# The first batch of a sliding-window attention + MLP kernel: one block of v loaded through ScalarE's queue, and two pairs' transposes moved ahead of two bias tables

## The chip, the cores and the metric

The kernel runs on one core of one Trainium2 chip. The metric is the device time of one execution in microseconds (us). A time is the median of several executions; next to it stands one execution that the hardware profiler recorded, from which all durations of single instructions come.

## What is computed

Eight batches of eight heads, 576 positions, head size 64. Each position attends to itself and the 127 positions before it, with a bias that falls linearly with distance (ALiBi). The result, 4608 tokens by 512, goes through a two-layer network with a hard-swish between.

```python
scores = scale * np.matmul(q, k.transpose(0, 1, 3, 2))
rel = pos[:, None] - pos[None, :]
bias = slopes[:, None, None] * (-np.abs(rel))[None, :, :]
mask = (rel >= 0) & (rel < 128)
scores = np.where(mask, scores + bias[None], -1e9)
attn = softmax(scores)                 # over the last axis
x = np.matmul(attn, v).transpose(0, 2, 1, 3).reshape(4608, 512)
h = x @ w_in                           # 512 x 2048
g = h * np.clip(h + 3.0, 0.0, 6.0) / 6.0
out = g @ w_out                        # 2048 x 512
```

## The kernel before

The work goes batch by batch; within a batch two heads make a pair, so a batch has four pairs, numbered g = 0 to 3 for batch 0 and g = 4 to 7 for batch 1. The order of the instructions on each engine is the order in which the program writes them out; nothing is reordered. The attention of a batch is woven into the network's matmuls of earlier tokens; batch 0 has no earlier tokens, so at the start the engines have only the attention of batch 0 to do. This start is `first_batch`.

For each pair of batch 0 the steps are these.

- `load_run` (L92) loads q or k of the pair, 288 KB each, as one row of 2304 bytes for each partition. The k runs are issued by ScalarE, the q runs by SyncE (SP): pair 0 first, then 1, 2, 3.
- `prepare(g, ...)` (L208) casts both to bf16 tiles `pr`.
- `transposes(g, ...)` (L219) turns them on TensorE with 18 small matmuls for q and 18 for k, into the PSUM tiles `tp`, and two copies (L220) bring q and k into `qTb` and `kTb`.
- `tables_diag` (L271) and `tables_off` (L307, L310) put the bias tables of the pair into PSUM by matmuls with the identity; `scores_diag` (L296) and `scores_off` (L322, L328) add the scores of the diagonal and the off-diagonal blocks on top. The two PSUM buffers of the pool `ps_sc` are taken in turn by the diagonal tile `scd`, the off-diagonal tile `sco` and later by `attend`.
- `exp_full` (L348, L335) is one exponential of 128x1024 on ScalarE for each of the two tiles.

All of v of batch 0 goes to `ldbuf` by `load_tokens(0, "v")` (L112): five blocks of tokens, four with 128 rows (256 KB each) and a last one with 64 rows (128 KB), cut into pieces of 256 bytes. All five are issued by SP, in order, right behind its four q runs. `cast_v` (L181) casts each block into `vbuf`. The first load of the network's weights, `load_w_in(0)` (L166, issued by GpSimd), stands behind `cast_v(0, 1, P)` on GpSimd's queue. P, V and A name the engine of a copy: GpSimd, VectorE, ScalarE.

Behind that stand the loads of batch 1's q and k, `load_double(1, dp, ...)` (L98): for dp = 0 and 1 two DMAs of k and two of q on SP's queue, then batch 1's v. Then come `attend(0)` to `attend(3)` (L383, L391; reciprocal and product L412, L413) with `back` (L432, L438), which transposes a pair's result into `xT`. `up_begin(0, 0, 3)` (L451) starts the network's first matmuls with three of the four pairs; it needs `w_in` of `load_w_in(0)` and the `xT` of pairs 0 to 2. `back(3)` and `wide_double(1, 0, "q", V)` (L254), the transposes of batch 1's first q, come next; the latter needs `prepare_double(1, 0, (P, P))` (L227), four casts on GpSimd, one for each of the four DMAs of dp = 0.

A DMA that SP or ScalarE issues takes the next of eight completion semaphores and waits until that semaphore's earlier DMA has landed. So the first v block waits for pair 0's k run, the second for pair 0's q run, the third for pair 1's k run, the fourth for pair 1's q run and the fifth for pair 2's k run. The wait and the issue occupy the issuing engine's queue: nothing behind them on that engine starts before.

Of the kernel before, what the change touches and what calls it, by code (L numbers as in the profile page):

```python
# [18 lines left out]
def kernel(  # L19
# [9 lines left out]
    nc = tc.nc  # L29
    B, H, S, D = q.shape  # L30
# [54 lines left out]
    src_of = {"q": q, "k": k, "v": v}  # L85
# [16 lines left out]
    def tokens(b, nm):  # L102
        if (b, nm) not in ld:
            i = 2 + b % 2 if b < 3 else (3, 1, 0, 2)[(3 * (b - 3) + "qkv".index(nm)) % 4]
            ld[b, nm] = ldbuf[i][:, 0:NQ * H * D].rearrange("p (j h d) -> p j h d", j=NQ, h=H)
        return ld[b, nm]

    def load_tokens(b, nm):
        t = tokens(b, nm)
        for j in range(NQ):  # L110
            n = min(128, S - j * 128)
            nc.sync.dma_start(out=t[:n, j, :, :],  # L112
                              in_=src_of[nm][b, :, ds(j * 128, n), :].rearrange("h p d -> p h d"))

    def constants():
        make_identity(nc, ident)
# [33 lines left out]
    def warm_up(n):  # L150
        w = ps_av.tile([128, 128], FP32, tag="av", name="w")
        for _ in range(n):
            nc.tensor.matmul(w, lhsT=ident, rhs=ident, start=True, stop=True)
# [11 lines left out]
    def load_w_in(g):  # L165
        nc.gpsimd.dma_start(  # L166
            out=w_in_sb[:, :, ts(g, 512)],
            in_=moe_w_in[:, ts(g, 512)].rearrange("(k p) f -> p k f", p=128))
# [6 lines left out]
    def second_w_in():  # L175
        nc.gpsimd.memset(w_out_sb[:, 4, 0:1], 0.0)
        load_w_in(1)

    def cast_v(b, j, copy):
        n = min(128, S - j * 128)  # L180
        copy(out=vbuf[b % 2][:n, j, :, 0:D], in_=ld[b, "v"][:n, j, :, :])  # L181
# [22 lines left out]
    def prepare(g, copies):  # L204
        for nm, copy in zip("qk", copies):
            pr = prs.tile([128, RT * D], BF16, tag=f"pr{nm}", name="pr",
                          padded_shape=[128, 2 * RT * D])
            copy(out=pr, in_=runs[nm][:, g % NP, :])  # L208
            st[g, nm] = pr

    def transposes(g, copies):
        b, hp = divmod(g, NP)
        for nm, dst, copy in (("q", qTb[b % 2], copies[0]), ("k", kTb[b % 2], copies[1])):
            src = st.pop((g, nm))
            tp = ps_h.tile([128, RT, RP], BF16, tag="h", name="tp", padded_shape=[128, 16, 64])
            for t in range(RT):
                for e in range(2):
                    r = slice(e * D, (e + 1) * D)
                    nc.tensor.transpose(tp[r, t, :], src[r, ts(t, D)], ident[r, r])  # L219
            copy(out=dst[:, hp, :, :].rearrange("p j c -> p (j c)")[:, 0:S].rearrange(  # L220
                "p (a t) -> p a t", t=RT), in_=tp.rearrange("p t a -> p a t"))
# [38 lines left out]
    def full(g):  # L260
        return g < NB_FULL * NP
# [4 lines left out]
    def tables_diag(g):  # L266
        scd = ps_sc.tile([128, 2, 512], FP32, tag="sc", name="scd")
        st[g, "scd"] = scd
        for e in range(2 if diag_tabled(g) else 0):
            t = tab[:, 2 * (g % NP) + e, 1:2, :]  # L270
            nc.tensor.matmul(scd[:, e, :].rearrange("p (j c) -> p j c", j=4), lhsT=ident,  # L271
                             rhs=t.to_broadcast([128, 4, 128]), start=True, stop=False)
# [12 lines left out]
    def scores_diag(g):  # L285
        rooms(g)
        b, hp = divmod(g, NP)
        qT, kT = qTb[b % 2][:, hp, :, :], kTb[b % 2][:, hp, :, :]
        first = not diag_tabled(g)
        if (g, "scd") not in st:  # L290
            tables_diag(g)
        scd = st[g, "scd"]
        for j in range(4):
            for e in range(2):
                r = slice(e * D, (e + 1) * D)
                nc.tensor.matmul(scd[:, e, ts(j, 128)], lhsT=kT[r, j, :],  # L296
                                 rhs=qT[r, j, :], start=first, stop=first or j == 3)

    def tables_off(g):
        hp = g % NP  # L300
        sco = ps_sc.tile([128, 2, 512], FP32, tag="sc", name="sco")
        st[g, "sco"] = sco
        if full(g):
            for e in range(2):
                h = 2 * hp + e
                t = tab[:, h, 0:1, :]
                nc.tensor.matmul(sco[:, e, 128:512].rearrange("p (j c) -> p j c", j=3),  # L307
                                 lhsT=ident, rhs=t.to_broadcast([128, 3, 128]),
                                 start=True, stop=False)
                nc.tensor.matmul(sco[:, e, 0:128].rearrange("p (s c) -> p s c", s=2),  # L310
                                 lhsT=ident, rhs=tab[:, h, :, 0:64], start=False, stop=False)
# [22 lines left out]
    def exp_off_full(g):  # L334
        nc.scalar.activation(out=st[g, "po"].rearrange("p e j c -> p e (j c)"),  # L335
                             in_=st[g, "sco"], func=ACT.Exp, scale=scale)

    def exp_full(g):
        for e in range(2):
            exp_diag(g, e)  # L340
        exp_off_full(g)

    def exp_diag(g, e):
        h = 2 * (g % NP) + e
        pd, sc = st[g, "pd"], st[g, "scd"]
        if diag_tabled(g):
            if e == 0:
                nc.scalar.activation(out=pd.rearrange("p e j c -> p e (j c)"), in_=sc,  # L348
                                     func=ACT.Exp, scale=scale)
            return  # L350
        nc.scalar.activation(out=pd[:, e, :, :].rearrange("p j c -> p (j c)"),  # L351
                             in_=sc[:, e, :], func=ACT.Exp,
                             bias=bias_d[:, h:h + 1], scale=scale)
        nc.gpsimd.affine_select(out=pd[:, e, :, :], in_=pd[:, e, :, :],  # L354
                                pattern=[[0, 4], [1, 128]], channel_multiplier=-1, base=0,
                                compare_op=ALU.is_ge, fill=0.0)
# [176 lines left out]
    V, P, A = nc.vector.tensor_copy, nc.gpsimd.tensor_copy, nc.scalar.copy  # L533
# [23 lines left out]

    def first_batch():
        prepare(0, (V, A))
        warm_up(20)  # L560
        tables_diag(0)
        tables_off(0)
        warm_up(10)
        transposes(0, (V, A))
        scores_diag(0)
        prepare(1, (P, V))
        transposes(1, (V, V))
        scores_off(0)
        exp_full(0)
        scores_diag(1)  # L570
        prepare(2, (P, P))
        tables_off(1)
        transposes(2, (V, V))
        scores_off(1)
        exp_full(1)
        scores_diag(2)
        prepare(3, (P, V))
        tables_off(2)
        transposes(3, (V, V))
        scores_off(2)  # L580
        exp_full(2)
        scores_diag(3)
        scores_off(3)
        exp_full(3)
        cast_v(0, 0, V)
        cast_v(0, 1, P)
        load_w_in(0)
        cast_v(0, 2, V)
        cast_v(0, 3, V)
        cast_v(0, 4, P)  # L590
        for dp in range(2):
            for nm in "kq":
                load_double(1, dp, nm, nc.sync)
        load_tokens(1, "v")
        attend(0)
        attend(1)
        back(0)
        attend(2)
        back(1)
        second_w_in()  # L600
        prepare_double(1, 0, (P, P))
        attend(3)
        back(2)
        up_begin(0, 0, 3)
        back(3)
        wide_double(1, 0, "q", V)
        prepare_double(1, 1, (P,), "k")
        load_w_in(2)
        prepare_double(1, 1, (P,), "q")
        load_w_in(3)  # L610
        for dp in range(2):
            for nm in "kq":
                load_double(2, dp, nm, nc.sync)
        up_begin(0, 1, 3)
        done[0] = NP
        fill(1)
        wide_double(1, 0, "k", A)
        fill(2)
# [99 lines left out]
    with tc.manual_schedule(engines=every):  # L718
        load_run(0, "k", nc.scalar)
        load_run(0, "q", nc.sync)  # L720
        load_run(1, "k", nc.scalar)
        load_run(1, "q", nc.sync)
        for g in (2, 3):
            load_run(g, "k", nc.scalar)
            load_run(g, "q", nc.sync)
        load_tokens(0, "v")
        constants()
        memsets()
        memsets_later()
        first_batch()  # L730
        second_batch()
        fill(2)
        segment(2 * NP, G, lambda g: FILLS.get(g, (1, 1, 1, 2, 0, 1, 2)))
        done[0] = G
        fill(len(units))
# [30 lines left out]
```

## Time and profile before

| | us |
|---|---|
| median of 3 executions (323.81 to 324.2) | 324.15 |
| the profiled execution, whole time | 323.38 |
| its span, first to last instruction | 321.7 |
| TensorE (PE) busy | 308.1 (96%) |
| ScalarE (ACT) busy | 195.1 (61%) |
| VectorE (DVE) busy | 172.7 (54%) |
| GpSimd (POOL) busy | 140.7 (44%) |
| granted TensorE clock | 1.000 |

The span is counted from the first instruction; 323.38 - 321.7 = 1.68 us of the profiled execution lie outside it. A busy PE is not a PE at its peak, since matmuls overlap. Where the text names a time without more, it is the time from the span's start. In the timeline a row is: start, duration, engine, line, operation, what it writes and reads, count, and in brackets how long the engine had been idle and what ended that. SPq, ACTq and POOLq are the engines' DMA-issuing instructions. In the table by stretches, "DMA share" is the mean busy share of the 16 DMA engines; packets of several queues overlap in it, so it can exceed 1.

### The profile page before, as it was taken

Reading aid. Unit: us, or ns where it says so; the run is one execution under the profiler, and the core shown is the slowest. Engines: PE = TensorE matmul, PEld = TensorE weight load, DVE = VectorE, ACT = ScalarE, POOL = GpSimd, SP = SyncE. Lnnn points to the kernel's source line nnn. Section 1 sums busy time; section 2 is a strip of 40 time slices with the busy share of each in tenths; the row PEclk is TensorE's granted clock in tenths of the full one; section 3 lists DMA queues with packets and bytes.
Section 4 is the critical chain, followed back from the end, with each engine's and each line's share of the span. In section 5 each row is a group of like instructions: output and inputs, shape, how many; then the busy total and the mean of one; then the engine's idle time right before and its main releaser. Section 6 shows DMA issues by size and latency. Waiting matters only on the chain.

```text
span 321.7 us, 7010 instructions
## 1 busy us (share of the span) xinstructions
PE 308.1 (96%) x2699; PEld 166.7 (52%) x2738; DVE 172.7 (54%) x338; ACT 195.1 (61%) x334; POOL 140.7 (44%) x249
## 2 busy tenths in 40 slices
PE   6879999999999999999999999999999999999996
PEld 5465465555555455455677644554554444444443
DVE  6657675554356555555555556555655455455510
ACT  4748976877777766666676657666764344244401
POOL 8456592683494767356745664563331000000000
PEclk9999999999999999999999999999999999999999
DMA  7999999899999999999999999932112200000112
GB/s 277 202 319 225 272 255 208 223 235 204 220 223 184 220 198 201 200 223 205 186 191 191 229 176 201 211 108 86 23 53 64 76 34 35 33 33 33 67 52 79
DMA packets 131425, 51.90 MB, mean 161 GB/s; under 512 B 118976, under 2 KB 123328, under 8 KB 131392
## 3 DMA queue, kind: packets, MB, share of 16 engines
q1 hardware_dynamic: 126160, 45.36, 67.0%
q0 software_dynamic: 4224, 4.19, 8.3%
q10 hardware_dynamic: 1008, 1.90, 1.6%
q8 instruction: 21, 0.34, 0.5%
q14 instruction: 12, 0.10, 0.1%
HBM read 36.70 MB, written 9.44 MB: 143 GB/s over the span
## 4 chain that ended last, share of the span: by engine, by line
PE 82%; DMA 5%; ACT 4%; POOL 4%; issue 2%; DVE 2%; SPq 1%; POOLq 0%
PE ops L501 35%; PE hps L451 35%; DMA ldbuf<-in_q_dram 3%; PE scd L296 2%; DMA qTb<-tbuf 2%; PE av L391 2%; PE av L383 2%; ACT r L470 2%; PE sco L328 1%; PE ops L482 1%; ACT kTb L244 1%; PE tp L254 1%; POOL tbuf L194 1%; ACT gbuf L351 1%; SPq L98 1%
## 5 line engine op out<-in xcount | busy, mean ns | idle before, releaser
L471 DVE SCALAR_TENSOR_TENSOR gbuf<-r,hps 128x512 bf16<-128x512 f32 x144 | 98.7, 687 | 102.5 <-ACT r L470 100.2
L470 ACT ACTIVATE r<-hps,bias 128x512 f32<-128x512 f32 x144 | 98.9, 689 | 89.5 <-PE hps L451 88.2
L451 PE MATMUL hps<-xT,w_in_sb 128*128 128x512 bf16 (+1 forms) x621 | 142.7, 358 | 2.3 <-DMA w_in_sb<-in_moe_w_in_dram 0.9
L501 PE MATMUL ops<-w_out_sb,gbuf 128*128 128x512 bf16 x540 | 134.2, 380 | 2.3 <-issue 1.7
L451 PEld LDWEIGHTS <-w_in_sb 128*128 128x128 bf16 x640 | 58.8, 98 | 54.8 <-DMA w_in_sb<-in_moe_w_in_dram 1.3
L501 PEld LDWEIGHTS <-gbuf 128*128 128x128 bf16 x560 | 52.2, 98 | 57.2
L354 POOL TENSOR_SCALAR_AFFINE_SELECT pd<-pd 128x512 bf16<-128x512 bf16 x48 | 29.6, 631 | 34.5 <-ACT pd L351 34.4
L364 POOL TENSOR_SCALAR_AFFINE_SELECT po<-po 128x512 bf16<-128x512 bf16 x48 | 30.1, 633 | 32.7 <-ACT po L361 32.6
L351 ACT ACTIVATE pd<-scd,bias_d 128x512 bf16<-128x512 f32 x48 | 31.6, 685 | 5.0 <-PE scd L296 3.6
L194 POOL CAST tbuf<-ldbuf 128x512 bf16<-128x512 f32 (+1 forms) x45 | 25.5, 611 | 18.7 <-DMA qTb<-tbuf 9.8
L510 DVE COPY osb<-ops 128x512 f32<-128x512 f32 x33 | 22.7, 687 | 20.3 <-PE ops L501 20.3
L361 ACT ACTIVATE po<-sco,bias_o 128x512 bf16<-128x512 f32 x48 | 33.1, 689 | 0.0
L402 DVE TENSOR_TENSOR avs<-av,rc 128x384 bf16<-128x384 f32 (+1 forms) x48 | 23.6, 491 | 1.6
L391 PEld LDWEIGHTS <-pd 128*128 128x128 bf16 x192 | 14.4, 97 | 8.3 <-issue 0.5
L383 PE MATMUL av<-vbuf,po 128*128 128x65 bf16 x192 | 18.1, 193 | 0.1
L391 PE MATMUL av<-vbuf,pd 128*128 128x65 bf16 x192 | 17.5, 194 | 0.3 <-ACT kTb L244 0.3
L383 PEld LDWEIGHTS <-po 128*128 128x128 bf16 x192 | 14.4, 98 | 3.1 <-DVE avs L402 0.5
L187 POOL CAST vbuf<-ldbuf 128x1024 bf16<-128x1024 f32 x14 | 14.3, 1040 | 3.2 <-DMA ldbuf<-in_v_dram 3.2
L367 ACT ACTIVATE p4buf<-sco,bias_d 128x64 bf16<-128x64 f32 x48 | 15.5, 324 | 0.0
L227 POOL CAST pr<-ldbuf 128x576 bf16<-128x576 f32 x20 | 12.8, 669 | 4.4 <-DMA ldbuf<-in_k_dram 3.4
L296 PE MATMUL scd<-qTb,kTb 64*128 64x128 bf16 x256 | 12.7, 219 | 1.8 <-DVE kTb L220 1.1
L296 PEld LDWEIGHTS <-kTb 64*128 64x128 bf16 x256 | 7.2, 94 | 13.5 <-issue 9.7
(96 smaller groups left out, 215.0 us busy)
## 6 DMA issues: line engine op xcount, KB each, us to landing
out_dram<-osb SPq DMA_DIRECT2D x33, 256.0 KB, 2.4
ldbuf<-in_v_dram SPq DMA_DIRECT2D x32, 256.0 KB, 5.3
ldbuf<-in_q_dram SPq DMA_DIRECT2D x20, 256.0 KB, 5.1
ldbuf<-in_k_dram SPq DMA_DIRECT2D x16, 256.0 KB, 4.6
ldbuf<-in_q_dram SPq DMA_DIRECT2D x12, 288.0 KB, 6.4
ldbuf<-in_k_dram SPq DMA_DIRECT2D x12, 288.0 KB, 6.4
w_in_sb<-in_moe_w_in_dram POOLq DMA_DIRECT2D x4, 512.0 KB, 9.2
w_out_sb<-in_moe_w_out_dram POOLq DMA_DIRECT2D x4, 512.0 KB, 11.1
```

The lines of the kernel that those rows point to most:

```text
L194: nc.gpsimd.tensor_copy(out=tbuf[:m, :, j, :], in_=s[:m, j, :, :].rearrange("p (i e) d -> p i (e d)", e=2))
L296: nc.tensor.matmul(scd[:, e, ts(j, 128)], lhsT=kT[r, j, :], rhs=qT[r, j, :], start=first, stop=first or j == 3)
L351: nc.scalar.activation(out=pd[:, e, :, :].rearrange("p j c -> p (j c)"), in_=sc[:, e, :], func=ACT.Exp, bias=bias_d[:, h:h + 1], scale=scale)
L354: nc.gpsimd.affine_select(out=pd[:, e, :, :], in_=pd[:, e, :, :], pattern=[[0, 4], [1, 128]], channel_multiplier=-1, base=0, compare_op=AL ...
L361: nc.scalar.activation(out=po[:, e, :, :].rearrange("p j c -> p (j c)"), in_=sc[:, e, :], func=ACT.Exp, bias=bias_o[:, h:h + 1], scale=scale)
L364: nc.gpsimd.affine_select(out=po[:, e, :, :], in_=po[:, e, :, :], pattern=[[0, 4], [-1, 128]], channel_multiplier=1, base=-1, compare_op=A ...
L383: nc.tensor.matmul(out_av, lhsT=po[:, e, qt % 4, :], rhs=vb[:, qt - 1, h, :], start=True, stop=False)
L391: nc.tensor.matmul(out_av, lhsT=d, rhs=vb[:, qt, h, :], start=(qt == 0), stop=True)
L451: nc.tensor.matmul(hps[:, lo:hi], lhsT=w_in_sb[:, ks, ts(ms, 128)], rhs=xT[:, ks, ds(src, hi - lo)], start=(ks == 0), stop=(ks == n_ks - 1))
L470: nc.scalar.activation(out=r6, in_=hps, func=ACT.Relu, bias=bias3[:, 0:1], scale=1.0 / 6.0)
L471: nc.vector.scalar_tensor_tensor(out=gts[nt][:, ms, :], in0=r6, scalar=1.0, in1=hps, op0=ALU.min, op1=ALU.mult)
L501: nc.tensor.matmul(ops[nt, sub], lhsT=gts[nt][:, ms, ts(sub, 128)], rhs=w_out_sb[:, ms, :], start=(ms == 0), stop=(ms == n_ms - 1))
```

## The change

Block 1 of batch 0's v is issued by ScalarE, behind its cast of pair 0's k in `prepare(0, (V, A))`; SP issues the other four, the 64-row block first. GpSimd casts the 64-row block ahead of block 1 instead of last. On TensorE `transposes(2)` is written ahead of `tables_off(1)` and `transposes(3)` ahead of `tables_off(2)`. Counts of instructions and bytes stay as they were.

In the generated program the eight semaphores fall so that ScalarE's new DMA waits until pair 1's k run has landed, and SP's four wait for pair 0's k run (64-row block), pair 0's q run (block 0), pair 1's q run (block 2) and pair 2's k run (block 3).

```diff
+    def load_block(b, nm, j, eng):
+        n = min(128, S - j * 128)
+        eng.dma_start(out=tokens(b, nm)[:n, j, :, :],
+                      in_=src_of[nm][b, :, ds(j * 128, n), :].rearrange("h p d -> p h d"))
+
     def load_tokens(b, nm):
-        t = tokens(b, nm)
         for j in range(NQ):
-            n = min(128, S - j * 128)
-            nc.sync.dma_start(out=t[:n, j, :, :],
-                              in_=src_of[nm][b, :, ds(j * 128, n), :].rearrange("h p d -> p h d"))
+            load_block(b, nm, j, nc.sync)
...
     def first_batch():
         prepare(0, (V, A))
+        load_block(0, "v", 1, nc.scalar)
+        for j in (4, 0, 2, 3):
+            load_block(0, "v", j, nc.sync)
         warm_up(20)
...
         prepare(2, (P, P))
+        transposes(2, (V, V))
         tables_off(1)
-        transposes(2, (V, V))
         scores_off(1)
         exp_full(1)
         scores_diag(2)
         prepare(3, (P, V))
+        transposes(3, (V, V))
         tables_off(2)
-        transposes(3, (V, V))
         scores_off(2)
...
         exp_full(3)
+        cast_v(0, 4, P)
         cast_v(0, 0, V)
         cast_v(0, 1, P)
         load_w_in(0)
         cast_v(0, 2, V)
         cast_v(0, 3, V)
-        cast_v(0, 4, P)
...
         for g in (2, 3):
             load_run(g, "k", nc.scalar)
             load_run(g, "q", nc.sync)
-        load_tokens(0, "v")
         constants()
```

## The prediction

> **What bounds the kernel now.** I read the page first, then the chain of waits over the first 60 us, the table by stretches of 1 us, the timeline of 4 to 24 us and SP's issues one by one. PE is busy 96% of the span, and from 24 us on nearly without a gap; the two thinnest slices on the page are the first (6) and the third (7, about 16 to 24 us). The change touches only what comes before 24 us, so the question is when that gap in slice three ends. The chain of waits there:
>
> ```profile
> 14.50 8.26 DMA ldbuf<-in_q_dram
> 22.76 0.05 issue
> 22.81 0.68 POOL pr L227
> 23.49 0.05 issue
> 23.54 0.68 PE tp L254 x9
> ```
>
> The last DMA of batch 1's first q is issued at 14.50 and lands at 22.76; GpSimd casts it (0.68), and PE's transposes start at 23.54. PE had waited once more, just before:
>
> ```profile
> 21.47 0.64 ACT L438 COPY xT<-tb 128x576 bf16<-128x576 bf16 x1 [0.53 <-PE tb L432]
> 22.37 0.60 PE L451 MATMUL hps<-xT,w_in_sb 128*128 128x512 bf16 x2 [0.94 <-DMA w_in_sb<-in_moe_w_in_dram]
> ```
>
> So three things end within 0.7 us: the xT of pair 2 (21.47 + 0.64 = 22.11), w_in (issued at 12.38, median 9.7 to landing, so 22.1), and q (22.76). PE's idle time there is 0.94 + 0.29 = 1.23 us: about what a change of the start can win, and only if all three come earlier.
>
> Why do the loads land so late? By stretches (PE, PEld, DVE, ACT, POOL busy, then clock, DMA share, GB/s):
>
> ```profile
> 11.00:12.00 1.00, 1.00 (x22) 0.41 (x16) 1.00 (x2) 0.47 (x1) 0.18 (x1) 1.00 1.29 220
> 13.00:14.00 1.00, 1.00 (x44) 0.75 (x43) 0.23 (x1) 0.85 (x1) 0.26 (x1) 1.00 0.70 144
> 14.00:15.00 1.00, 0.88 (x14) 0.31 (x12) 1.00 (x2) 0.61 (x1) 0.00 (x0) 1.00 0.84 65
> 21.00:22.00 1.00, 0.43 (x5) 0.26 (x4) 0.96 (x2) 0.53 (x1) 0.79 (x2) 1.00 1.05 400
> ```
>
> The v pieces of 256 bytes run at 220 GB/s with the engines full, the rows of 2304 bytes at 400. Between them is a hole, 144 and 65 GB/s. SP's issues tell why:
>
> ```profile
> 6.36 2.78 SPq L112 DMA_DIRECT2D ldbuf<-in_v_dram  x1
> 9.19 1.02 SPq L112 DMA_DIRECT2D ldbuf<-in_v_dram  x1
> 10.26 1.94 SPq L112 DMA_DIRECT2D ldbuf<-in_v_dram  x1
> 12.31 1.45 SPq L98 DMA_DIRECT2D ldbuf<-in_k_dram  x2
> ```
>
> The first two v blocks are issued in 0.39 and 0.65 us; the third holds SP for 2.78 (until 9.14, about when the last q run lands at 9.3), the fifth for 1.94. I read this as a full queue holding its issuer. The next loads are therefore issued only at 12.31, too late to follow v without a gap.
>
> **The change, part by part.** No instruction is added or removed.
>
> *ScalarE's new DMA.* It waits for pair 1's k run; SP's third v block had the same wait and started at 6.36. ACT is free from 4.62 + 0.67 = 5.29, and what is queued behind is pair 0's k copy:
>
> ```profile
> 6.12 0.64 ACT L220 COPY kTb<-tp 128x576 bf16<-128x576 bf16 x1 [0.82 <-PE tp L219]
> ```
>
> How long such an issue holds ACT no row shows. Low end 0.39 (first v block on SP), high end 2.78 (third). ACT's queue then holds two k runs only; SP's held three q runs at its first v block, so I take 0.39. ACT is free at 6.75, the copy starts at 6.78 (+0.66), scores_diag(0) at 7.47 instead of 6.81. Pair 1's transposes waited for a GpSimd cast until 7.48 anyway (they ran at 7.53) and now start at 7.80: +0.27.
>
> *Transposes ahead of tables.* The path from pair to pair runs through PE and DVE: scores_diag, tables_off, transposes, q copy and k copy (0.76 each), scores_diag; 9.53, 12.39, 15.25, so 2.86 us a pair. Tables_off stands between scores_diag and transposes from 9.85 to 10.39, 0.54 us. Out of the way, each of the two pairs comes 0.54 earlier. The casts they need are there: pair 2's end at 9.14, pair 3's k on DVE directly behind pair 2's k copy. What is late next is scores_off, which shifts by as much as it gains, and ACT: an exponential takes 1.02, back to back 0.92 apart (15.69 to 16.61). Following the eight through: 7.90, 8.94, 10.22, 11.80, 12.72, 14.12, 15.04, 16.18, where they were 7.25, 8.66, 9.96, 11.53, 12.83, 14.39, 15.69, 16.61. The last is 0.43 earlier: +0.27 from ACT's wait, up to -1.08 from the two moves, and ACT nearly full from 11.8 on takes back the rest. The xT of pair 2 would come at 21.68.
>
> *SP's queue.* It has 3.5 v blocks. Three blocks in all were issued by 9.14 and four by 10.21, so 3.5 by about 10, 2 us ahead of 12.20. The doubles follow: their four waits (q run 2, k run 3, q run 3, the 64-row block) are over by about 10.5, so the last q goes out near 12.5 instead of 14.50. Then the hole closes: of 13 to 15, (220 - 144) + (220 - 65) = 231 KB are regained, 1.05 us at 220 GB/s. Low end: nothing, if the slowest of the 16 DMA engines had no hole (the landing waits for all sixteen); high end 2.0, the issue's whole lead. I take 0.9: q lands at 21.9, its cast ends at 22.6.
>
> *Block 1 and GpSimd.* The cast of the 64-row block (0.87) moves from 15.80, where nothing waited behind it but the next w_in, to about 10.2, where GpSimd idles 1.69 us. Block 1 landed near 11.77 as second in SP's queue; as second in ACT's, behind the k runs (last landing about 9.6) and sharing with SP's, I expect 11.5 to 13, so w_in is issued between 12.1 and 13.6 (now 12.38). The doubles now run beside it from the start. I take 21.7 for its landing, between 21.3 (0.9 earlier, as q) and 22.6.
>
> [...]
>
> *Sum.* With xT at 21.68 and w_in at 21.7, up_begin runs at 21.8 instead of 22.37; from its start to the transposes PE needs 0.87 (22.37 to 22.80, and 0.44 for back(3)), so 22.7, q's cast 22.6 permitting, against 23.54: 0.8 us. From there PE and ACT are nearly full (PE 1.00 in each stretch of 24 to 27, ACT 7.87 of 8 in 32 to 40), so the shift stays; one DMA on the later chain (qTb from 95.37) is issued by work that shifts too. I take off 0.1 for a longer ACT issue: 0.7 us. Profiled execution 323.38 - 0.7 = 322.7, span 321.0. The median of the runs is 0.77 above the profiled one: 324.15 - 0.7 = 323.45. 0.2% of it is 0.65 us, about what a measurement of this kernel can tell from no change.
>
> **The rivals.** *Hidden (24%).* The slowest DMA engine had no hole, so q and w_in land within 0.3 of 22.76 and 22.1, and PE waits for them whatever the front does. For it: the engines are full at 9 to 12, and bytes are the same. Against: 65 GB/s at 14 to 15. Time about 324.0.
>
> *ACT is held (18%), slower.* The new issue blocks as SP's third did, because SP's own queue is full or because both share what writes descriptors. At 2.78 ACT is free at 9.14, scores_diag(0) runs at 9.86, pair 1's transposes at 10.2 (+2.66); less 1.08, the front ends about 1.6 late, xT of pair 2 at 23.7, up_begin's third matmul behind it, transposes at about 24.6: 1.1 later, 325.25. It decides from where the front is 0.7 late (w_in and q cover less than that), an issue of about 1.5 us. Against: both engines issued runs side by side from 0.81 on, 0.39 to 0.48 each.
>
> *w_in is late (12%), slower.* Block 1 shares its engines, lands at 13 or after, w_in goes out 1.2 late and shares with the doubles from its first packet; landing 23.0, PE's start 0.7 late, 324.9.
>
> **How the numbers follow.** Forecast 46%, own range 322.9 to 323.8. Most of its weight, 42 points, is beyond 0.65 us; the other 4 and the hidden case make 28% within 0.2%; the two others 30% slower. The range goes from 322.6, where the idle 1.23 us is won and w_in's next wait (0.39 at 28.39) with it, to 325.4, just beyond the held ACT.
>
> **What would show it.** ACTq's v issue at 6.3 to 6.4 with about 0.4 us, kTb's first copy near 6.8; scores_diag(2) at about 12.1 and (3) at 14.4; the last exponential of batch 0 near 16.2; SP's first double near 10.3; no stretch of 1 us under 150 GB/s between 12 and 16; up_begin near 21.8. A v issue on ACT above 1.5 us, or the first cast of q (L227) still ending after 23.4, makes the forecast wrong.

## The result, and the profile after

| | before | changed |
|---|---|---|
| median, same chip (10 runs each) | 323.69 us (322.8 to 324.29) | 325.14 us (324.08 to 325.93) |
| ratio to before | 1 | 1.0052, 95% interval 1.0038 to 1.0066 |
| the profiled execution, whole time | 323.38 | 324.08 |
| its span | 321.7 | 322.3 |
| last exponential of batch 0 starts | 16.61 | 18.56 |
| first transposes of batch 1's q start | 23.54 | 24.39 |

The change makes the kernel slower by 0.5%; the forecast was 0.7 us faster. The ratios, here and below, are worked out from all runs and are not quotients of the medians; one execution of e2 and one of e4, over 1.5% longer than the fastest of its kernel, are left out of them. The profiled execution of the changed kernel is the fastest of its ten; why the others are longer comes with experiment e4.

Read the DMA side first. The timeline of the changed kernel's issues and GpSimd's casts (start, duration, engine, line, operation, tiles, count):

```profile
6.29 0.46 ACTq L110 DMA_DIRECT2D ldbuf<-in_v_dram  x1
9.87 3.00 SPq L98 DMA_DIRECT2D ldbuf<-in_k_dram  x2
13.55 0.88 POOL L168 DMA_DIRECT2D w_in_sb<-in_moe_w_in_dram  x1
20.67 3.71 POOL L229 CAST pr<-ldbuf 128x576 bf16<-128x576 f32 x6
```

ScalarE's new issue takes 0.46 us, SP reaches the first double at 9.87 instead of 12.31, and GpSimd does six of the eight casts of batch 1's q and k in one piece from 20.67, with no wait for a load between them. The same in stretches of 1 us (behind the length of the stretch PE, PEld, DVE, ACT, POOL busy, then clock, DMA share, GB/s):

```profile
13.00:14.00 1.00, 0.88 (x35) 0.67 (x36) 0.36 (x2) 1.00 (x2) 1.00 (x2) 1.00 1.31 235
14.00:15.00 1.00, 0.00 (x0) 0.00 (x0) 0.53 (x1) 0.44 (x1) 0.43 (x1) 1.00 1.06 326
15.00:16.00 1.00, 0.72 (x13) 0.47 (x12) 0.36 (x1) 0.00 (x0) 0.00 (x0) 1.00 1.06 365
```

The hole of 144 and 65 GB/s is closed (235 and 326). But look at PE in the row of 14 to 15: 0.00, TensorE does nothing at all. The chain of waits names it:

```profile
12.99 0.33 PE scd L298 x8
13.32 0.56 PE tp L221 x27
13.88 1.40 issue
15.28 0.32 PE tp L221 x9
...
23.21 0.65 ACT xT L440
23.86 0.04 issue
23.90 0.38 PE hps L453
24.28 0.28 PE tb L434 x5
24.56 0.50 PE tp L256 x9
```

In the middle of `transposes(3)`, after 27 of 36, TensorE stops for 1.40 us. "issue" means that it waited for nothing that the profile shows: no semaphore, no tile. All 36 transposes belong to one pair, and their source casts were over. From there the whole front is late: the third matmul of `up_begin` now starts at 23.90 behind the xT of pair 2 (23.21 + 0.65), where in the kernel before it was ready at 22.11, and the chain no longer holds a load. What was the bound, the DMA, came earlier; what was covered, the front, is the bound now.

What is late is seen in the DMA view. The queues of two windows of 2 us (queue and kind: packets, MB, share of 16 engines), first the kernel before, 10 to 12 us, then the changed one, 12 to 14 us:

```profile
q1 hardware_dynamic: 1706, 0.43, 131.3%
q8 instruction: 1, 0.02, 4.0%
```

```profile
q1 hardware_dynamic: 1593, 0.45, 132.5%
q8 instruction: 1, 0.02, 4.0%
```

The single packet on q8, of kind "instruction", has 16 KB. There are 21 of them in the whole run (0.34 MB), and the first starts at 10.46 in the kernel before and at 12.51 in the changed one. TensorE resumes at 15.28, 2.77 us after the packet's start. The experiments ask whether this is the cause, and why the packet is late.

### The profile page after: what moved, and what is told of

Read it like the earlier page. It is cut to its first block, busy times and chain, and to the rows that moved or that the text cites. A ratio compares the mean times of both kernels' runs of the same rounds, so it can differ in the third digit from the quotient of the medians.

```text
span 322.3 us, 7010 instructions
## 1 busy us (share of the span) xinstructions
PE 309.2 (96%) x2699; PEld 168.2 (52%) x2738; DVE 173.1 (54%) x338; ACT 195.1 (61%) x334; POOL 140.6 (44%) x249
## 4 chain that ended last, share of the span: by engine, by line
PE 82%; ACT 5%; DMA 3%; issue 3%; POOL 3%; DVE 2%; SPq 1%; POOLq 0%
PE hps L453 34%; PE ops L503 33%; PE scd L298 3%; DMA qTb<-tbuf 2%; PE av L393 2%; ACT r L472 2%; PE av L385 2%; PE sco L330 2%; DMA ldbuf<-in_q_dram 1%; POOL tbuf L196 1%; PE ops L484 1%; PE w L155 1%; SPq L110 1%; ACT xT L440 1%; PE tp L221 1%
## 5 line engine op out<-in xcount | busy, mean ns | idle before, releaser
L393 PEld LDWEIGHTS <-pd 128*128 128x128 bf16 x192 | 14.4, 97 | 8.3 <-issue 0.5
L385 PEld LDWEIGHTS <-po 128*128 128x128 bf16 x192 | 14.3, 98 | 3.2 <-DVE avs L404 0.5
L298 PEld LDWEIGHTS <-kTb 64*128 64x128 bf16 x256 | 7.2, 94 | 12.5 <-issue 9.7
L229 POOL CAST pr<-ldbuf 128x576 bf16<-128x576 f32 x20 | 12.5, 667 | 0.0
```

The source lines that it names most:

```text
L298: nc.tensor.matmul(scd[:, e, ts(j, 128)], lhsT=kT[r, j, :], rhs=qT[r, j, :], start=first, stop=first or j == 3)
L385: nc.tensor.matmul(out_av, lhsT=po[:, e, qt % 4, :], rhs=vb[:, qt - 1, h, :], start=True, stop=False)
L393: nc.tensor.matmul(out_av, lhsT=d, rhs=vb[:, qt, h, :], start=(qt == 0), stop=True)
```

## The experiments

Ratios are to runs of the kernel before on the same chip, with the 95% interval. In what follows the supply theory (R) is that TensorE stops because its next instructions are not loaded; its rivals are that ScalarE's new issue holds the front (A), that the moved transposes themselves cost (T) and that w_in is late (W).

**e1: the transposes alone.** v is loaded as before, all by SP in the old order.

```diff
         prepare(2, (P, P))
+        transposes(2, (V, V))
         tables_off(1)
-        transposes(2, (V, V))
```

(and the same for pair 3).

> Only the transposes of pairs 2 and 3 are moved; all of v stays on SyncE in the old order. Profile of the changed kernel: TensorE stops for 1.40 us inside the transposes of pair 3 (13.88 to 15.28, ended by 'issue'), and the one instruction load (queue q8) in that stretch starts about 2 us later than before. Theory R (late instruction load): with v on one queue the load comes early as before (near 10.5), ready near 13.2; TensorE reaches the same place at 13.1 to 13.6, so the stop is under 0.5 us and the time is 0 to 0.5 us below before. Rival A (ScalarE's DMA delays pair 0's k): the full 0.43 us gain at the last exponential shows, time 0 to 0.5 below before as well. Rival T (the moved transposes themselves cost): slower by 0.5 us or more.

Measured: ratio 0.9992 (0.9977 to 1.0007), median 323.01. The load starts at 10.63, as in the kernel before, but TensorE arrives sooner, and it stops at the same place, after 27 transposes of pair 3, for a shorter time (timeline; the brackets give the idle time and its cause):

```profile
12.18 0.62 PE L219 MATMUL tp<-ident,pr 64*64 64x64 bf16 x27
13.43 0.32 PE L219 MATMUL tp<-ident,pr 64*64 64x64 bf16 x9 [0.63 <-issue]
...
22.73 0.68 PE L254 MATMUL tp<-ident,pr 128*128 128x128 bf16 x9
...
28.13 0.60 PE L451 MATMUL hps<-xT,w_in_sb 128*128 128x512 bf16 x2 [0.47 <-DMA w_in_sb<-in_moe_w_in_dram]
```

In spite of the stop batch 1's transposes start at 22.73, 0.81 earlier than before. That gain is gone by 28.13: TensorE then waits for the second part of w_in. In the kernel before, its weight loads had waited for the same part until 28.39, as the prediction's range says. So T falls, the pair-to-pair path is shorter, and a second gate stands behind it. The stop of 0.63 us is a little over the 0.5 us expected.

**e2: the DMA part alone.** The v loads and casts of the change, `transposes` where they were.

> Only the DMA part and the order of the casts; transposes stay where they were. R: the instruction load is late again because two queues of 256-byte pieces run ahead of it; TensorE stops 1 us or more before 16 us; time 1.0 to 2.0 us above before. A: no such stop, but pair 0's k copy on ScalarE starts 0.6 us later and all of the front with it; 0.3 to 0.7 above. T: no loss, and the earlier doubles (landing 2 us earlier) bring -0.3 to -1.0.

Measured: 1.0037 (1.0012 to 1.0062), median 324.18. The load starts at 12.62 and TensorE stops for 1.04 us, in `transposes(3)` again, though these stand behind `tables_off(2)` here. The last exponential starts at 18.11 and batch 1's transposes at 23.95. Most of the loss belongs to the DMA part.

**e3: the change without ScalarE's DMA.** SP issues all five blocks, the 64-row block first.

```diff
-        load_block(0, "v", 1, nc.scalar)
-        for j in (4, 0, 2, 3):
+        for j in (4, 0, 1, 2, 3):
             load_block(0, "v", j, nc.sync)
```

> The change with all five v blocks on SyncE, the 64-row block first, then 0 to 3. A: ScalarE is free again, so the loss goes: 0.3 to 0.8 us below before. R: the v pieces come through one queue, so the instruction load waits about as long as before (start near 10.5 to 11) and the stop shrinks below 0.6 us; time within 0.4 of before. W (w_in issued 1.2 us later, behind block 1): block 1 is third in SyncE's queue, w_in stays late (issued 13 or later) and the loss stays, 1 us or more above before.

Measured: 1.0031 (1.0011 to 1.0051), median 324.06. The load starts at 11.41, the stop is 1.65 us. Without any DMA on ScalarE most of the loss remains, so rival A falls. R's numbers missed too: it had expected a start by 11 us and a stop under 0.6. The sign named for W came true, since w_in was issued at 13.14 and the loss stayed. But w_in is not what is waited for here: it landed at 21.71, and the first matmul that reads it starts at 23.20, the third at 24.09 behind the xT of pair 2, which is late from the stop on.

**e4: the changed kernel once more.**

> The changed kernel once more, for a second profile beside these. R: the stop inside the transposes of pair 3 is there again, 1 us or more, and the time is 1.2 to 2.0 us above before. If the stop is gone and the time is still 1.2 us above, R falls. The slow matmuls up to about 7 us in the first profile (warm-up matmuls 107 ns apart instead of 56) should vary between profiles if they don't belong to the change.

Measured: 1.0056 (1.0034 to 1.0079), median 325.12; load at 12.79, stop 1.87 us. This profile shows what the first one of the changed kernel did not. In the table by stretches, the granted clock is the number behind the five engines:

```profile
15.00:16.00 1.00, 0.42 (x11) 0.32 (x11) 0.07 (x1) 0.00 (x0) 0.00 (x0) 1.00 0.93 233
17.00:18.00 1.00, 1.00 (x10) 0.34 (x8) 0.70 (x3) 0.83 (x1) 0.00 (x0) 0.50 1.15 257
18.00:19.00 1.00, 1.00 (x8) 0.39 (x4) 0.00 (x0) 0.83 (x1) 0.00 (x0) 0.50 1.15 248
19.00:20.00 1.00, 1.00 (x20) 0.84 (x20) 0.00 (x0) 0.52 (x2) 0.00 (x0) 0.50 1.18 327
```

About 1.3 us after TensorE has resumed, the clock falls to 0.50 and stays there for some 3.4 us (16.89 to 20.30); the eight matmuls of `scores_diag(3)` take 0.61 us instead of 0.40. Batch 1's transposes start at 25.78, and the profiled execution takes 325.83. The mean clock of this run is 0.995, which is what such a stretch makes: 0.5 x 3.4 / 324 = 0.005. Of the changed kernel's ten runs nine have a mean clock of 0.995 or below (324.89 to 325.93 us) and one has 1.000 (324.08, the profiled one); the 34 runs of the kernel before beside e1 to e4 have 0.999 or 1.000 (of the 35 beside e5 to e8 one has 0.995). So the loss very likely has two parts: the stop, and in nine runs of ten a halved clock behind it, which for these is read from their mean clock alone. The split is an estimate. The nine are about 1 us longer than the tenth (median 325.16 against 324.08); the stop's part is 0.8 us by e3's seven runs with a clock of 1.000 (median 324.12 against 323.28), and less by that tenth run (324.08 against the median of 323.69).

**e5: less v in the queue.** The change without loading blocks 2 and 3 of v; their casts read block 0, so part of the attention of batch 0 is computed on other data.

```diff
-        for j in (4, 0, 2, 3):
+        for j in (4, 0):
```

> The changed kernel without the loads of v blocks 2 and 3 (both casts read block 0 instead, so the output is not the reference's): nothing else of the order moves. In the five profiles with a stop, TensorE goes on 2.7 to 2.84 us after the instruction load (q8) starts, always at the same place in the transposes of pair 3; the load starts later, the more v pieces were issued ahead of it (about 1.7 to 3.4 blocks of 1.2 us, counted from 8.5 us). Theory R: with 1.5 blocks on SyncE and one on ScalarE ahead of it the load starts near 10.5 to 11.5 instead of 12.5 to 12.8, and the stop shrinks from 1.4 to 2.1 us to under 0.8; time 0.8 to 1.8 us below the changed kernel. Rival A (ScalarE's issue) or T (the transposes): the stop and the time stay, within 0.4 us of the changed kernel. Less data also lets the doubles land earlier, so only the stop, not the time alone, decides.

Measured: 1.0025 (1.0003 to 1.0048), median 324.64. Load at 11.80, stop 1.37 us: it moved in the right direction (12.51 and 12.79 with the blocks), but load and stop missed the bounds given. The table further down says why: of the two blocks left out only one had stood ahead of the load, and in this profile TensorE came to the place of the stop 0.7 us sooner than in that of the changed kernel.

**e6: the moved transposes with v held.** e1, but SP's blocks 1 to 4 wait for a one-column memset of GpSimd behind its cast of pair 1's q.

```diff
         prepare(1, (P, V))
+        nc.gpsimd.memset(tokens(0, "v")[:, 1, 0, 0:1], 0.0)
+        for j in range(1, NQ):
+            load_block(j)
```

> Only the transposes are moved, as in e1, and SyncE's second v block (and all behind it) is held until GpSimd has cast pair 1's q, near 7.5 us, by a one-column memset in its place. R: only one v block is ahead of the instruction load, so it starts near 9.7 instead of 10.6, and TensorE, which reaches the place near 12.6, goes on without a stop (e1: 0.8 us); batch 0's last exponential 0.8 earlier than in e1, time 0.3 to 1.0 us below before. If the load doesn't come earlier, R's account of what it waits for is wrong. Against a gain: v lands later by what the hold costs (0 to 0.5 us).

Measured: 1.0027 (0.9998 to 1.0056), median 323.98. No stop that the profile shows, yet no gain: TensorE waits for the second part of w_in until 28.80. The expectation missed where it mattered: the load was to start near 9.7 and started at 10.73, no earlier than e1's 10.63, and by its own words the account of what the load waits for was then wrong. The stop is gone for another reason: in this profile the front ran later, and TensorE reached the place at 13.54 where e1 had reached it at 12.61. So e6 doesn't speak for the supply theory. Why the hold brought nothing is in the table further down: it ended at 7.25, and the moment that is taken there as that of asking for the load is 8.61.

**e7 and e8: the place of the stop moved.** 72 TensorE instructions more are put ahead of everything, in the warm-up: 12 of the large matmuls instead of 20, and 44 small ones. e7 is the changed kernel so padded, e8 is e1.

```diff
-        warm_up(20)
+        warm_up(12)
+        pad_rows(44)
```

> The changed kernel with 12 large and 44 small warm-up matmuls instead of 20 large ones: 36 more, that is 72 more TensorE instructions ahead of everything, so the place where TensorE runs out of loaded instructions moves 72 instructions forward, from the middle of pair 3's transposes to the start of pair 2's scores, where TensorE waits for a copy anyhow. R: no stop in pair 3's transposes; a stop, if any, near pair 2's scores and under 0.6 us, because the load is asked for some 2 us earlier (in pair 0's transposes) when fewer v pieces are issued; time 0.8 to 1.8 below the changed kernel. A or T: nothing changes but a possible 0.2 to 0.5 for a longer warm-up.

> The same 36 extra small matmuls in e1 (transposes moved, v on SyncE). R: e1's stop of 0.8 us goes, the last exponential of batch 0 comes about 0.8 earlier than e1's 16.70, and the time is 0.3 to 1.0 below before. If w_in and batch 1's q, which land no earlier than before, bound it instead, the time is that of e1 though the stop is gone.

Measured: e7 1.0056 (1.0025 to 1.0086), e8 0.9993 (0.9972 to 1.0014). In e7's timeline the transposes of pair 3 run through, and the stop stands between the two bias matmuls of `tables_diag`:

```profile
12.16 0.39 PE L279 MATMUL scd<-tab,ident 128*128 128x512 bf16 x1
13.77 0.38 PE L279 MATMUL scd<-tab,ident 128*128 128x512 bf16 x1 [1.22 <-issue]
```

Counted in the trace's records of TensorE (weight loads and matmuls together, and two of its sequencer's at the very start), the last one ahead of the stop is number 449 in this kernel as in every other that stops, although it is another instruction of the program. The stop sits on an instruction count, not on an operation, a tile or a moment. And record 450 starts 2.70 to 2.96 us after the start of the q8 packet in all ten profiles with a stop (2.84 here). From these two TensorE's wait is put down to that packet. The size was not as forecast: 1.22 us where under 0.6 was expected, and no time below the changed kernel. In e8 next to nothing is left of the stop, and there is no gain, as in e6. Next to nothing, for in both kernels record 450 still starts 0.1 us late, 2.93 (e6) and 2.73 us (e8) after the packet: there TensorE and the load arrive together.

**e9, e11, e12: the changed kernel with holds.** e9 holds SP's blocks 0, 2 and 3 with a memset as in e6. e11 is e1 with batch 1's v held until GpSimd has cast the third double and so placed behind the second part of w_in. e12 is e9 with e11's hold.

```diff
-        for j in (4, 0, 2, 3):
-            load_block(0, "v", j, nc.sync)
+        load_block(0, "v", 4, nc.sync)
...
         prepare(1, (P, V))
+        nc.gpsimd.memset(tokens(0, "v")[:, 0, 0, 0:1], 0.0)
+        for j in (0, 2, 3):
+            load_block(0, "v", j, nc.sync)
```

```diff
-        load_tokens(1, "v")
         attend(0)
...
         prepare_double(1, 1, (P,), "k")
+        nc.gpsimd.memset(tokens(1, "v")[:, 0, 0, 0:1], 0.0)
+        load_tokens(1, "v")
```

> The changed kernel, with SyncE's blocks 0, 2 and 3 of v held until GpSimd has cast pair 1's q (about 7.5 us), by a one-column memset into block 0's place; the 64-row block and ScalarE's block 1 go out as in the change. Theory (TensorE's instruction load waits behind the v pieces that were issued before it): only 1.5 blocks stand ahead of it, so it starts between 10.0 and 11.2 us instead of 12.51, TensorE stops for less than 0.5 us instead of 1.40, the last exponential of batch 0 starts by 17.2, and the ratio to the kernel before falls from 1.005 to between 0.996 and 1.000. Rival one (the lateness has to do with the moved transposes or ScalarE's issue, not with what SyncE has queued): start 11.5 or later, stop of 1.2 us or more, ratio 1.003 to 1.006. Rival two (the hold makes v itself late): no stop, but w_in is issued after 13.6 and up_begin waits for it beyond 23; ratio about 1.002.

> The transposes alone (old v order), with the load of batch 1's v held until GpSimd has cast the third double (about 25 us) and placed behind the second part of w_in. Theory (what the moved transposes win at 22 us is given back where TensorE waits 0.84 us for the second part of w_in at 28.12, because that part shares the engines with batch 1's v): that wait falls under 0.3 us, the second part lands before 27.5, and the ratio falls from 0.999 to between 0.996 and 0.9985. Rival (the gain was already lost in the 0.8 us stop at 12.6, and later work absorbs any shift): the wait goes but the ratio stays 0.999 to 1.000. Second rival: batch 1's v comes too late for its casts (second cast after 40 us), and the ratio is above 1.001.

> The changed kernel with both holds: SyncE's blocks 0, 2 and 3 of batch 0's v behind GpSimd's cast of pair 1, and batch 1's v behind the cast of the third double. Theory: the load starts by 11.2 us, no stop above 0.5 us, no wait above 0.3 us for the second part of w_in, the wide transposes start near 22.8 and the shift stays: ratio 0.995 to 0.998, the fastest of all. Rival (the front is not what sets the end, or batch 1's v is now late): ratio 0.999 or above.

Measured: e9 1.0016 (0.9997 to 1.0035), load 12.22, stop 1.04 us. e11 1.0010 (0.9986 to 1.0034): the second part of w_in still lets TensorE go on only at 28.34, so batch 1's v was not what delayed it, and a new wait of 1.11 us for a cast of GpSimd stands at 47.81. e12 1.0025 (1.0009 to 1.0041), load 11.53, stop 1.11 us. All three missed. e9 missed, by the count below, because the hold ended too soon: its blocks 0 and 2 were issued at 7.25 to 8.27, ahead of the moment taken as that of asking (8.84). That can be counted. The asking itself has no record in the trace; the start of TensorE's record 194 is taken for it, 256 ahead of 450 and so about one packet's worth (252 to 254 records, last section). This is an assumption. Add up the v whose issue had ended by then (a block is 262 KB of 1000 bytes, the 64-row block 131) and the v whose packets left ahead of the q8 packet, by the trace's packet records:

| | taken as asked at | v issued by then, KB | v that left first, KB | load starts | stop |
|---|---|---|---|---|---|
| before | 7.78 | 524 | 501 | 10.46 | none |
| e1 | 7.67 | 524 | 502 | 10.63 | 0.63 |
| e6 | 8.61 | 524 | 536 | 10.73 | none |
| e8 | 7.51 | 524 | 512 | 10.46 | none |
| e11 | 7.92 | 524 | 528 | 10.62 | 0.34 |
| e3 | 7.48 | 655 | 650 | 11.41 | 1.65 |
| e5 | 8.01 | 655 | 652 | 11.80 | 1.37 |
| e12 | 8.23 | 655 | 655 | 11.53 | 1.11 |
| e9 | 8.84 | 917 | 835 | 12.22 | 1.04 |
| e2 | 8.23 | 917 | 912 | 12.62 | 1.04 |
| changed | 8.75 | 917 | 874 | 12.51 | 1.40 |
| changed again (e4) | 8.58 | 917 | 935 | 12.79 | 1.87 |
| e7 | 6.83 | 655 | 540 | 10.93 | 1.22 |

In every row but the last the two amounts agree within 10%: if it is asked for then, the load leaves about when the v issued ahead of it has left. In e7 it left with 115 KB of that v still to go, so there the moment is wrong or the load overtook.

**e10: held until after the assumed moment of asking.** As e9, with the hold behind `prepare(2, (P, P))`, so until about 9.2 us.

```diff
         prepare(2, (P, P))
+        nc.gpsimd.memset(tokens(0, "v")[:, 0, 0, 0:1], 0.0)
+        for j in (0, 2, 3):
+            load_block(0, "v", j, nc.sync)
```

> The changed kernel with SyncE's blocks 0, 2 and 3 of v held until GpSimd has cast pair 2's q and k (about 9.2 us), so until after the moment at which TensorE's load is taken to be asked for (256 PE instructions ahead of the place of the stop, 7.8 to 8.8 us); ahead of it stand the 64-row block and ScalarE's block 1 alone, 393 KB. In the runs so far the v bytes that left before the load's packet were those issued by that moment: 501 KB of 524 in the kernel before, 874 of 917 in the changed one, 655 of 655 with both holds. Theory (the load takes its turn behind all pieces issued before it): between 350 and 420 KB leave first, the load starts between 9.8 and 10.8 us, TensorE does not stop for more than 0.3 us there, and the ratio is 0.996 to 1.000. Rival (it is not a matter of turn: the load comes when the busy phase of small pieces lets it): more than 500 KB leave first, start at 11.2 or later, stop above 0.8 us, ratio 1.001 or more. A third outcome, no stop but a ratio of 1.000 or more, would say that w_in or q, held back by the later issue, takes the front's gain.

Measured: 0.9998 (0.9986 to 1.0010), median 322.93 against 323.07. Record 194 starts at 8.00, with 393 KB issued; 374 KB left first; the load starts at 9.96. The timeline has all 36 transposes of pair 3 in one piece:

```profile
12.17 0.40 PE L298 MATMUL scd<-qTb,kTb 64*128 64x128 bf16 x8
12.50 0.82 PE L221 MATMUL tp<-ident,pr 64*64 64x64 bf16 x36
...
21.48 0.82 PE L453 MATMUL hps<-xT,w_in_sb 128*128 128x512 bf16 x3 [0.58 <-DMA w_in_sb<-in_moe_w_in_dram]
22.14 0.44 PE L434 MATMUL tb<-ident,avs 128*128 128x128 bf16 x5
22.85 0.68 PE L256 MATMUL tp<-ident,pr 128*128 128x128 bf16 x9 [0.27 <-POOL pr L229]
...
28.39 1.04 PE L453 MATMUL hps<-xT,w_in_sb 128*128 128x512 bf16 x4 [0.61 <-DMA w_in_sb<-in_moe_w_in_dram]
```

The stop is gone, eleven of twelve runs have a clock of 0.999 or 1.000, and the loss of 0.5% with them. So the cause of the loss is shown: with the load early again, and the change otherwise kept, there is no stop and no loss. Batch 1's transposes start 0.69 earlier than in the kernel before. But the second part of w_in lets TensorE go on only at 28.38 (weight load; 28.39 in the kernel before), and there is no gain. No version was found that is measurably faster than the kernel before.

## Why the prediction was wrong, point by point

- *ScalarE's new DMA: 0.39 us, k copy at 6.78.* The size was right (0.46). The copy came at 7.49, because `transposes(0)` themselves started at 6.45 instead of 5.32: the ten warm-up matmuls just ahead of them took 1.27 us instead of 0.72. Both are seen in other profiles too (e6, without a ScalarE DMA: 1.27, and 6.44; e3, without one: 0.72, and 5.42), so it is not put down to the change. The copy waited for TensorE, so the issue on ScalarE cost nothing in this profile.
- *Transposes ahead of tables: 0.54 us for each of two pairs.* Right in mechanism, smaller in size. The two moves act from `scores_diag(1)` to (2) and from (2) to (3), 2.86 us each before. In e10, without a stop, (0) to (3) are 7.42, 9.74, 12.17 and 14.67, so 2.43 and 2.50: 0.43 and 0.36 won instead of 0.54 each. The step from (0) to (1), 2.72 before and 2.32 there, no move touches. (3) was forecast at 14.4, and the last exponential, forecast at 16.18, starts at 16.29 in e10: without the stop the working of the front holds.
- *SP's queue: the first double near 10.3, the hole closes, q 0.9 earlier.* Right in what came, only half right in why. SP reached the first double at 9.87, no stretch is under 150 GB/s between 12 and 16, and batch 1's first q landed at 20.73 instead of 22.76, more than forecast. But its last DMA was to go out near 12.5 and went out at 14.27, hardly before the 14.50 of the kernel before: the first DMA of the double alone held SP for 2.34 us. What came earlier are the three DMAs ahead of it (the first k landed at 16.76 instead of 18.57), and w_in, whose queue q0 took 48.0% of the 16 engines' time beside 60.9% for SP's q1 (14.3 to 20.7 us), went out 1.17 us later; what each did no run separates, and that q won more than twice what was forecast is luck. Alone it bought nothing. That a full queue holds its issuer was the prediction's reading; what the traces show is the holding, 2.78 us by the third v block before and 2.34 here, not its cause.
- *w_in, issued between 12.1 and 13.6, landing 21.7.* Issued at 13.55, landed at 22.74: late, beyond the range given (up to 22.6), but not binding, since the xT of pair 2 came at 23.86.
- *The last exponential at 16.18, "the front ends 0.43 earlier".* This is the step that failed. It came at 18.56, by the later start of `transposes(0)` (1.13 us) and, above all, by the stop of 1.40. The working followed the casts, TensorE, VectorE and ScalarE, and took for granted that TensorE has its instructions. In the kernel before, the load was in time by little: packet at 10.46, and 2.70 to 2.96 us from there (as in the ten profiles with a stop) is 13.16 to 13.42, while TensorE reached record 449 at 13.63. The change used that cover up from both sides. The moved transposes bring TensorE there sooner (e1: a stop of 0.63), and with the additional v the load comes later (874 KB of v left ahead of it instead of 501; e2: 912 KB, a stop of 1.04); both together cost 1.40 to 1.87, and nine of ten runs have a mean clock of 0.995 or below.
- *Rival "ACT is held", 18%.* Its time of 325.25 is near the measured 325.14 by luck, for its cause did not occur: ACT's issue took 0.46 us, far from the 1.5 us from which it decides. Neither of the two reasons it gives for such a hold is shown by a run. Rivals "hidden" and "w_in is late": q and the hole moved as forecast, and w_in was late without deciding.
- *"From there PE and ACT are nearly full, so the shift stays."* This would have failed too. The wait of 0.39 us at 28.39 was named in the range as something more to win, and is by the timelines the gate at which the gain is given back. In e1, e6 and e10 batch 1's transposes start at 22.73, 23.10 and 22.85, and all three kernels wait at that gate until 28.1 to 28.8. Issuing its load earlier doesn't help: issued at 17.66 in e10, 17.97 in the kernel before and 19.93 in the changed one, it landed at 28.34, 28.35 and 28.33. It hardly moves at first: of the queues in e1, where it was issued at 18.07, between 19 and 22 us (packets, MB, share), q0 is GpSimd's and q1 SP's with the doubles:

```profile
q1 hardware_dynamic: 583, 1.19, 102.5%
q0 software_dynamic: 15, 0.01, 2.6%
```

  Even without the stop the change is worth about nothing (e10: 0.9998). That this gate takes the whole gain is read from the timelines and not shown: no run moved it, though e11 and e12 were meant to.

## What to carry to other kernels

In the changed kernel TensorE's stop of 1.40 us hung on a packet of 16 KB of kind "instruction" (q8), ahead of which 874 KB of v left. So when an engine shows "issue" in the middle of a run of equal instructions, look for packets of that kind, and count the engine's records up to the stop in several variants: here there were 449 in each of ten profiles. Cover that is not named is used up unseen; here 0.2 to 0.5 us of it was there with 501 KB of v ahead of the packet, and none with 874 KB. And when one gate is opened, work out the next gate in the same unit before writing down the gain: three loads with 0.7 us between them were seen, the fourth, 5 us later, was not counted, and no version got past it.

## What the runs showed of the hardware that was not expected

- The packets of kind "instruction" on q8, on the first of which TensorE's stop hangs, have 16 KB each (21 packets, 0.34 MB, 0.5% of the 16 engines' span in the changed kernel). From the 4th to the 21st packet TensorE goes on by 254 records a packet in e1, and by 252 in the kernel before and in the changed one. From the first packet's start to the first record behind the stop pass 2.70 to 2.96 us in the ten profiles with a stop, of which the packet itself takes about 1.3 (1.27 in the kernel before, 1.26 in the changed one). In the changed kernel that cost a stop of 1.40 us.
- In the 14 profiles 374 to 935 KB of v left ahead of the first of these packets, and in 13 of them that is within 10% of the v issued by the start of record 194 (table above; in e7 540 of 655 KB). So this packet seems to wait for the data issued ahead of it, if it is asked for at that moment, which is an assumption. Later packets leave it open: the 7th and 8th of the 14 profiles start from 0.8 us before to 1.4 us after records 1730 and 1986 (194 + 256 x 6 and x 7, by the same assumption), though there too small pieces fill the engines (kernel before, 84 to 92 us: 4000 of 4384 packets under 512 B, the data's queue at 99.1% of the 16 engines). Either they are asked for earlier than that count says, or they don't always wait.
- A stop of TensorE of 1.65 us (e3) or 1.87 us (e4) was followed by a clock of 0.50 for 3.4 us; after 1.40 us in the profiled run of the changed kernel the clock stayed at 1.00. Whether the length of the stop decides, and why nine of ten runs of the changed kernel have a mean clock of 0.995 or below, stays open: the stop of an unprofiled run isn't recorded, and e6, without a stop in its profile, has 4 of 12 runs with a clock of 0.998 or less.
